# Attention, experts and a gated layer in one kernel: earlier weight loads, routing products in the score banks, one more copy on VectorE, and rows that hold columns and logits together

## The chip, the cores and the metric

The kernel runs on one core of a Trainium2 chip. The metric is device time in microseconds (us) of one execution. Five queues of instructions run side by side and each keeps its own order: TensorE (PE), VectorE (DVE), ScalarE (ACT), GpSimd (POOL) and SyncE (SP, which here only issues transfers). Instructions wait for each other through semaphores, so a late instruction holds everything behind it on its own queue.

## The reference

Three layers in a row, all in fp32:

```python
def _attn_ref(q, k, v, s):                      # B, H, S, D = 4, 8, 576, 64
    scores = scale * np.matmul(q, k.transpose(0, 1, 3, 2))
    cum = np.cumsum(np.maximum(s, 0.0), axis=-1)
    bias = -(cum[:, :, :, None] - cum[:, :, None, :])
    scores = np.where(causal, -1e9, scores + np.minimum(bias, 0.0))
    attn = np.exp(scores - scores.max(-1)); attn /= attn.sum(-1) + 1e-09
    return np.matmul(attn, v)
def _moe_ref(x, w_gate, w1, w2):                # 2304 tokens, 512 wide, 8 experts of 1024
    logits = x @ w_gate; expert_idx = np.argmax(logits, axis=1)
    ...                                         # gate_w: softmax of the chosen expert
    out[mask] = gate_w * (np.maximum(xe @ w1[e], 0.0) @ w2[e])
def _moe2_ref(x, w1, w2, w3, w_out):            # 768 wide
    return np.maximum(np.maximum(x @ w1, x @ w2), x @ w3) @ w_out
```

## The kernel before

The program has three stages. **Attention** goes over 16 pairs of heads (4 batches, 4 pairs each). Each pair has 576 query rows: four blocks of 128 for each of the two heads, and the last 64 rows of both heads together in one block of 128 partitions (the tiles `nst`, `Pt`, `tsum`). **The experts** follow: tokens are grouped by expert, gathered from the DRAM tensor `xd` and multiplied by weights that arrive in pieces of 128 x 1024 fp32; a piece is loaded (`wr`), rounded to its high half by ACT (L185) and the rest is taken by DVE (L681). **The second layer** comes last.

The order of the attention stage is written out as numbers. Every step is put into a heap at a slot by `at(slot, fn)`, and popping the heap writes the instructions; a slot is no time, only a place in the order. One pair has IT = 25 slots, and `SEQ` gives the place of each of its steps: `A0 B0 A1 B1 C2 C3 TT` are transposes of the exponentials into a PSUM bank "b" (L368) and their copies into `ptT` (L408 on DVE, L410 on ACT), `s0` to `s9` are scores into banks "a" (L302; L322 for the last rows), `v0 v1` are the products with the values into banks "c" (L420), `x0 x1` are the products with `rh` (L455), which give 128 columns of the output and 16 partial logits for each of five row tiles. There are 4 banks "a", 2 "b" and 2 "c", and each kind is used in turn, so a new product waits until the instruction that reads the bank's last product is done.

In a period PE works on three pairs: it transposes the exponentials of pair p-1 and multiplies them with the values, makes the scores of pair p, and makes the rows of pair p-2. DVE adds the bias and takes the minimum of each row (L308, L329), ACT takes the exponentials (L315, L337) out of three `ns` buffers. The bias of a pair, `bl` (two buffers), is loaded by SP from `cumd`, and POOL cuts the causal mask into it (L262, L267, L273).

After the last pair of each batch a list of some 33 small steps, `route`, follows at a spacing of RS slots. It sums the partial logits (L493), finds the expert, counts ranks by products with triangular and all-ones matrices (`r1`, L508 to L512, read by L516) and places token numbers by another product (`r3`, L539, read by L543). Both products of the first three batches use a bank "c".

Three weight pieces are placed inside the attention stage: `hi = WE1 + WES * n`, so at slots 80, 126 and 172, with the load WE0 slots from it and the rest (L681) WEL slots behind it.

Of the kernel before, what the change touches and what calls it, by code (L numbers as in the profile page):

```python
# [9 lines left out]
F32 = mybir.dt.float32  # L10
# [13 lines left out]
P = 128  # L24
WN = 128
# [32 lines left out]
BCE = "VAVAA"  # L58
LR, LE, LH, LL, LV, LK, LX = 2.5, 5.5, 1.5, 4.0, 1.0, 1.5, 1.5
NSB, PPB = 3, 4  # L60
# [14 lines left out]
WLO = "V"  # L75
WE0, WE1, WES, WEL, WEH = -15, 80, 46, 15, "A"
WHE, WLE = "A", "V"
# [13 lines left out]
       "v1": 9.1}  # L91
TDVE = ("A1", "B1")


def emit(nc, tc, qt, kt, v, s, wg, w1, w2, m64, out, dbg=None):
# [12 lines left out]
    cumd = dp.tile([B * H, BW], F32, name="cumd")  # L108
    xd = dp.tile([NT, DM], F32, name="xd")
    w32 = dp.tile([9, P, 1024], F32, name="w32")  # L110
# [12 lines left out]
    V.tensor_tensor_scan(cum, sn, sn, 0.0, ALU.add, ALU.max)  # L123
    cs = ab.tile([B * H, CW], F32, tag="hlv", name="cs", bufs=2)
# [4 lines left out]
    chl = ab.tile([B * H, 2, S], F32R, tag="hlv", name="chl", bufs=2)  # L129
    V.tensor_scalar(chl[:, 0], cum, 1.0, 1.0, ALU.mult, ALU.mult)  # L130
# [150 lines left out]
    xr = {}  # L281
    lp = {}

    def scores(p, slots):
# [76 lines left out]
        at(t + LE, tex)  # L361
        at(t + LE + 1, tnorm)

# [74 lines left out]
    def xrow(p, slots):  # L438
        d = st[p]
        b, h = divmod(2 * p, H)  # L440

        def begin():
            if h == 0:
                xr[b] = ab.tile([P, 5, DM], F32, tag="xr", name="xr", bufs=2)
                lp[b] = ab.tile([P, 5, H, NE], F32, tag="lp", name="lp", bufs=1)
                V.memset(lp[b][64:128, 4], 0.0)
            rc = d["rc"] = ab.tile([P, 5, 2], F32, tag="rc", name="rc", bufs=2)
            V.tensor_scalar(rc, ssum[b][:, :, h:h + 2], 1e-9, None, ALU.add)
            V.reciprocal(rc, rc)

        def mm(t0, t1):
            px = d["px", t0] = bank("c")
            for t in range(t0, t1):
                c = 144 * (t - t0)
                T.matmul(px[:, c:c + 144], d["oT"][:, 128 * t:128 * t + 128], rh[:, h // 2, :], start=True, stop=True)  # L455

        def ev(t0, t1):
            nt = t1 - t0
            pv = d["px", t0][:, :nt * 144].rearrange("p (t w) -> p t w", t=nt)
            for sl, ta, tb in (((slice(0, P)), t0, min(t1, 4)), ((slice(0, 64)), 4, t1)):  # L460
                if tb <= ta:
                    continue
                n = sl.stop
                pw = pv[sl, ta - t0:tb - t0]
                rr = d["rc"][sl, ta:tb, :].rearrange("p t (g o) -> p t g o", o=1)
# [12 lines left out]
    def route(b, t0):  # L478
# [25 lines left out]
        def r1():  # L504
            ohb = z["ohb"]
            z["pr"] = bank("b" if b == B - 1 else "c")
            prv = z["pr"][:, :5 * NG]
            T.matmul(prv, tri, ohb.rearrange("p t e -> p (t e)"), start=True, stop=False)  # L508
            for t in range(4):
                n = 4 - t  # L510
                T.matmul(prv[:, NG * (t + 1):], one, bc(ohb[:, t:t + 1, :], (P, n, NG)), start=False, stop=False)
            T.matmul(prv, one, bc(ocb.rearrange("p (o e) -> p o e", o=1), (P, 5, NG)), start=False, stop=True)  # L512

        op(r1)
        op(lambda: A.activation(sm([P, 5, NE], "ex"), z["ls"], AF.Exp))
        op(lambda: V.tensor_tensor(sm([P, 5, NG], "rv"), z["pr"][:, :5 * NG].rearrange("p (t e) -> p t e", t=5), oh,  # L516
# [39 lines left out]
    def constants():  # L556
        for g in range(2):
            V.tensor_copy(rh[64 * g:64 * g + 64, :, 64 * g:64 * g + 64],
                          bc(idf[64 * g:64 * g + 64, 64 * g:64 * g + 64].rearrange("p (o d) -> p o d", o=1), (64, H // 2, 64)))
        for tf, ti in late:  # L560
            V.tensor_copy(tf, ti)
# [17 lines left out]
    for g in range(2):  # L579
        at(6, lambda g=g: A.dma_start(rh[64 * g:64 * g + 64, :, 128 + 8 * g:136 + 8 * g],  # L580
                                        wg.rearrange("(h g d) e -> g d h e", g=2, d=64)[g]))
# [269 lines left out]
    def overflow():  # L851
        why = "bounded by the counts of the tokens"
        op = tc.alloc_tile_pool(name="op", bufs=1, side="right", reuse_waits="tile")
        with tc.If(nwin["n"] > 0):
            with tc.For_i(0, nwin["n"], 1) as i:
# [5 lines left out]
                SP.dma_start(ix, idd[ds(st_, WN)])  # L861
                x = op.tile([WN, DM], F32, name="x")
# [368 lines left out]
```

## Time and profile before

| | |
|---|---|
| median of 3 runs (lowest to highest) | 832.94 us (829.03 to 835.2) |
| the profiled execution | 829.74 us, of it a span of 827.9 us |
| PE busy | 765.1 us, 92% of the span |
| DVE, ACT, POOL busy | 431.1, 346.5, 110.9 us |
| PE busy from 0 to 240 us (attention and the change to the experts) | 200.0 of 240.0 us |
| PE busy from 240 us to the end | 565.1 of 587.9 us |

The attention stage ends at about 222 us. Up to there PE has holes; behind it PE is busy almost all the time. The profile names for each hole which engine's instruction ended it, and that is what has to be read.

### The profile page before, as it was taken

What the parts mean: (1) busy time and instruction counts of PE and PEld (TensorE: products, weight loads), DVE (VectorE), ACT (ScalarE), POOL (GpSimd) and SP (SyncE); (2) the same over time, 40 slices, a digit from 0 to 9 for tenths busy, and PEclk for the clock granted to TensorE, in tenths of its full rate; (3) what the DMA queues carried; (4) which work ended last, traced back from release to release, by engine and by line L of the source; (5) the groups of instructions that cost most, each with busy time, mean ns of one, the idle gap of its engine ahead of it and who ended that gap; (6) DMA issues with size and microseconds to landing.
All of it is one profiled execution on the core that took longest, in us unless ns stands there. A gap on an engine that the chain in (4) does not pass through costs nothing. (4 is left out here: it accounts for less than half of the span.)

```text
span 827.9 us, 13233 instructions
## 1 busy us (share of the span) xinstructions
PE 765.1 (92%) x4910; PEld 687.8 (83%) x4910; DVE 431.1 (52%) x1185; ACT 346.5 (42%) x804; POOL 110.9 (13%) x230
## 2 busy tenths in 40 slices
PE   7887778888889898898999999999999999999996
PEld 4565556556689898898899999998999999899995
DVE  5556465748567776777889944542222312223120
ACT  4766466567646444334554544522121211212111
POOL 3332132323412100200110000001000010100001
PEclk9999999999999999899999999999999999999998
DMA  6775856758258687867867742501000010100001
GB/s 177 204 187 144 238 126 177 193 162 238 78 185 290 229 282 257 283 228 255 295 232 240 228 152 81 178 2 38 1 26 13 1 39 1 38 1 9 30 1 39
DMA packets 36047, 115.47 MB, mean 139 GB/s; under 512 B 4921, under 2 KB 5003, under 8 KB 34059
## 3 DMA queue, kind: packets, MB, share of 16 engines
q1 hardware_dynamic: 25259, 85.27, 34.4%
q10 hardware_dynamic: 7456, 18.89, 6.5%
q0 software_dynamic: 3264, 10.42, 3.6%
q8 instruction: 40, 0.66, 0.3%
q14 instruction: 28, 0.23, 0.1%
HBM read 98.56 MB, written 16.01 MB: 138 GB/s over the span
## 5 line engine op out<-in xcount | busy, mean ns | idle before, releaser
L1127 DVE TENSOR_TENSOR mA<-ps_a,mA 128x384 f32<-128x384 f32 x72 | 40.2, 558 | 175.8 <-PE ps_a L935 175.8
L935 PE MATMUL ps_a<-yc,wq 128*128 128x384 f32 x720 | 126.9, 334 | 0.0
L935 PEld LDWEIGHTS ps_a<-yc,wq 128*128 128x128 f32 x720 | 125.2, 188 | 0.4
L935 PE MATMUL ps_c<-h,wq 128*128 128x336 f32 (+1 forms) x672 | 103.3, 310 | 9.5 <-ACT yT L981 5.5
L935 PEld LDWEIGHTS ps_c<-h,wq 128*128 128x128 f32 x672 | 97.9, 188 | 11.2 <-ACT yT L981 6.1
L935 PE MATMUL ps_a<-yc,wm 128*128 128x384 f32 x576 | 101.8, 334 | 0.0
L935 PE MATMUL ps_a<-xT,wq 128*128 128x336 f32 (+1 forms) x648 | 100.3, 314 | 0.1
L935 PEld LDWEIGHTS ps_a<-yc,wm 128*128 128x128 f32 x576 | 100.0, 188 | 0.0
L935 PEld LDWEIGHTS ps_a<-xT,wq 128*128 128x128 f32 x648 | 96.5, 193 | 0.4 <-DVE h L960 0.3
L315 ACT ACTIVATE P<-ns,mn 128x512 f32<-128x512 f32 (+3 forms) x128 | 70.6, 557 | 12.1 <-DVE mn L308 12.0
L935 PE MATMUL ps_c<-wm,g 128*128 128x512 f32 x324 | 74.7, 390 | 0.0
L1131 ACT ACTIVATE g<-mA 128x384 fp32r<-128x384 f32 x36 | 19.0, 527 | 132.9 <-DVE mA L1127 132.9
L935 PEld LDWEIGHTS ps_c<-wm,g 128*128 128x128 f32 x324 | 60.7, 188 | 12.4
L420 PE MATMUL ps_c<-ptT,nv 128*64 128x320 f32 (+4 forms) x448 | 50.8, 364 | 20.5 <-ACT ptT L410 19.2
L420 PEld LDWEIGHTS ps_c<-ptT,nv 128*64 128x64 f32 x448 | 29.6, 136 | 46.2 <-ACT ptT L410 27.0
L308 DVE CUSTOM_DVE_ANT_0 ns<-ps_a,bl 128x512 f32<-128x512 f32 (+3 forms) x128 | 57.4, 487 | 19.6 <-ACT P L315 9.3
L1150 POOL DMA_INDIRECT out<-o,midi x18 | 17.6, 976 | 373.3 <-ACT o L1146 366.3
L681 DVE TENSOR_TENSOR wq<-wr,wq 128x1024 fp32r<-128x1024 f32 x46 | 56.1, 1220 | 18.9 <-ACT wq L185 17.6
L185 ACT ACTIVATE wq<-wr 128x1024 fp32r<-128x1024 f32 x46 | 48.5, 1057 | 38.3 <-DMA wr<-in_w 33.9
L368 PE MATMUL ps_b<-idf,P 128*128 128x128 f32 x320 | 47.3, 288 | 8.0 <-ACT ptT L410 6.9
L410 ACT ACTIVATE ptT<-ps_b 128x512 f32<-128x512 f32 (+1 forms) x96 | 43.4, 505 | 19.3 <-PE ps_b L368 19.3
L302 PE MATMUL ps_a<-nk,nq 64*128 64x512 f32 (+3 forms) x256 | 48.1, 479 | 1.7 <-DVE mn L308 1.7
(222 smaller groups left out, 980.3 us busy)
## 6 DMA issues: line engine op xcount, KB each, us to landing
wr<-in_w SPq DMA_DIRECT2D x62, 512.0 KB, 4.6
bl<-cumd SPq DMA_DIRECT2D x30, 528.0 KB, 8.4
dr<-in_m ACTq DMA_DIRECT2D x24, 512.0 KB, 4.2
xr<-in_w SPq DMA_DIRECT2D x18, 512.0 KB, 3.9
nq<-in_qt SPq DMA_DIRECT2D x16, 352.0 KB, 3.4
nv<-in_v SPq DMA_DIRECT2D x16, 320.0 KB, 9.2
nk<-in_kt SPq DMA_DIRECT2D x16, 288.0 KB
w<-dc ACTq DMA_DIRECT2D x18, 256.0 KB, 4.7
```

The lines of the kernel that those rows point to most:

```text
L185: A.activation(o, x, AF.Copy)
L302: T.matmul(d["sp", i, g][:, :w], d["q"][r, 128 * i:128 * i + 128], d["k"][r, :w], start=True, stop=True)
L308: V.tensor_tensor_reduce(out=ns[:, :w], in0=d.pop(("sp", i, g))[:, :w], in1=d["bl"][:, 1024 * g + BOFF[i]:1024 * g + BOFF[i] + w], scale=- ...
L315: A.activation(pp, d.pop(("ns", i, g))[:, :w], AF.Exp, bias=d["mn"][:, c:c + 1], scale=-1.0, accum_out=ssum[b][:, i, h + g:h + g + 1])
L368: T.transpose(pt[:, c:c + 128], (d["P", "t"] if g == "t" else d["P", g, i])[:, k0:k0 + 128], idf)
L410: A.activation(f(d["pt"]), src, AF.Copy)
L420: T.matmul(po[64 * g:64 * g + 64, qa - c0:c1 - c0], d["v"][:, g, j], d["pt"][:, g, POFF[j] + qa - 128 * j:POFF[j] + c1 - 128 * j], start=( ...
L681: (V if eng == "V" else G).tensor_tensor(t[:, 1], raws.pop(key), t[:, 0].bitcast(F32), ALU.subtract)
L935: T.matmul(ps_, w_(zw), x_(zx), start=(first and n == 0), stop=(last and n == 2))
L1127: V.tensor_tensor(m, pm[:, :CH], m, ALU.max)
L1131: A.activation(t[:, 0], h2[c, f, "m"], AF.Copy)
L1150: G.indirect_dma_start(out, bass.IndirectOffsetOnAxis(ap=midi[:, n:n + 1].bitcast(U32), axis=0), h2.pop((c, x, "s")), None)
```

## The change

Four edits. The early weight pieces are loaded 62 slots ahead of their split in place of 15, and their rest is taken 3 slots behind it in place of 15. The routing products `r1` and `r3` of the first three batches go to a bank "a". The copy of `TT` (the last rows' transposes) is made by DVE in place of ACT. The row tile `xr` is 576 wide: for each pair of heads 8 logits, 128 columns, 8 logits; so one multiplication per bank takes columns and logits together, `lp` is gone, and the rows in `xd` and the gathered rows are 576 wide. The step that normalises the last rows stands 3.5 slots behind their exponential in place of 1. Three small tiles change the buffers that they share (`cs`, `chl`, `xw`).

```diff
+HW = 72
+XW = 8 * HW
-WE0, WE1, WES, WEL, WEH = -15, 80, 46, 15, "A"
+WE0, WE1, WES, WEL, WEH = -62, 80, 46, 3, "A"
-TDVE = ("A1", "B1")
+TDVE = ("A1", "B1", "TT")
-    xd = dp.tile([NT, DM], F32, name="xd")
+    xd = dp.tile([NT, XW], F32, name="xd")
...
-        at(t + LE + 1, tnorm)
+        at(t + LE + LN, tnorm)
...
-            pv = d["px", t0][:, :nt * 144].rearrange("p (t w) -> p t w", t=nt)
-            for sl, ta, tb in (((slice(0, P)), t0, min(t1, 4)), ((slice(0, 64)), 4, t1)):
...
-                V.tensor_tensor(xr[b][sl, ta:tb, 64 * h:64 * h + 128].rearrange("p t (g d) -> p t g d", g=2),
-                                pw[:, :, 0:128].rearrange("p t (g d) -> p t g d", g=2), bc(rr, (n, tb - ta, 2, 64)), ALU.mult)
-                V.tensor_tensor(lp[b][sl, ta:tb, h:h + 2, :], pw[:, :, 128:144].rearrange("p t (g e) -> p t g e", g=2), bc(rr, (n, tb - ta, 2, NE)),
-                                ALU.mult)
+            rr = d["rc"][:, t0:t1, :].rearrange("p t (g o) -> p t g o", o=1)
+            V.tensor_tensor(xr[b][:, t0:t1, HW * h:HW * h + 144].rearrange("p t (g w) -> p t g w", g=2),
+                            d["px", t0][:, :nt * 144].rearrange("p (t g w) -> p t g w", t=nt, g=2),
+                            bc(rr, (P, nt, 2, HW)), ALU.mult)
...
-        op(lambda: V.tensor_reduce(sm([P, 5, NE], "L"), lp[b].rearrange("p t h e -> p t e h"), AX.X, ALU.add))
+        for g, nm in enumerate(("L", "L1")):
+            o = g * (HW + D)
+            op(lambda o=o, nm=nm: V.tensor_reduce(
+                sm([P, 5, NE], nm), xr[b].rearrange("p t (m w) -> p t w m", w=2 * HW)[:, :, o:o + NE], AX.X, ALU.add))
+        op(lambda: V.tensor_tensor(z["L"], z["L"], z["L1"], ALU.add))
...
-            z["pr"] = bank("b" if b == B - 1 else "c")
+            z["pr"] = bank("b" if b == B - 1 else "a")
...
-            pg = z["pg"] = bank("b" if b == B - 1 else "c")
+            pg = z["pg"] = bank("b" if b == B - 1 else "a")
...
-                    T.transpose(pt[:, 0:WN], x[:, P * kk:P * kk + P], idf[0:WN, 0:WN])
+                    T.transpose(pt[:, 0:WN], heads(x, kk), idf[0:WN, 0:WN])
...
+    def heads(x, kk):
+
+        return x[:, 2 * HW * kk + NE:2 * HW * kk + NE + P]
```

How the order moves, at three places. **DVE, in the period in which the first batch's routing begins** (`ISA ns` is L308's minimum of a block, `ISA nst` that of the last rows, `mn` its read-out, `r_L` the logits). Before:

```order
L308 ISA ns,mn<-ps_a,bl 128x128
L308 ISA mn 128x1
L681 TENSOR_TENSOR wq_997<-wr_902,wq_997 128x1024
L494 TENSOR_REDUCE r_mx<-r_L 128x5
L495 TENSOR_TENSOR r_ls<-r_L,r_mx 128x40
L496 TENSOR_SCALAR r_val<-r_ls 128x40
L329 ISA nst,mn<-ps_a,bl 128x256
```

Now:

```order
L489 TENSOR_REDUCE r_L<-xr 128x40
L311 ISA ns,mn<-ps_a,bl 128x128
L311 ISA mn 128x1
L311 ISA ns,mn<-ps_a,bl 128x128
L311 ISA mn 128x1
L489 TENSOR_REDUCE r_L_1095<-xr 128x40
L491 TENSOR_TENSOR r_L<-r_L,r_L_1095 128x40
L411 COPY ptT<-ps_b 128x2x4x64
L492 TENSOR_REDUCE r_mx<-r_L 128x5
L332 ISA nst,mn<-ps_a,bl 128x256
```

The copy of `TT` stands between the last blocks' minima and the last rows' minima, in every period; in a period with routing, sums of logits stand ahead of it. The rest of the weight piece has left this place: it now stands ahead of the first minimum of the same period.

**PE, at the rank product of the second period of routing** (`rh,oT` are the row products, `nk,nq` the scores). Before:

```order
L508 LDWEIGHTS tri
L508 MATMUL ps_c<-r_ohb,tri 128x50
...
L512 LDWEIGHTS one
L512 MATMUL ps_c<-ocb,one 128x50
...
L455 MATMUL ps_c<-rh,oT 128x144 x5
L302 MATMUL ps_a<-nk,nq 128x384 x2
```

Now:

```order
L456 MATMUL ps_c<-rh,oT 128x144 x3
L506 LDWEIGHTS tri
L506 MATMUL ps_a<-r_ohb,tri 128x50
...
L510 LDWEIGHTS one
L510 MATMUL ps_a<-ocb,one 128x50
L456 MATMUL ps_c<-rh,oT 128x144 x2
L305 MATMUL ps_a<-nk,nq 128x384 x2
L305 MATMUL ps_a<-nk,nq 128x128 x2
```

The rank product left the ring of two banks "c" and entered the ring of four banks "a", in which the fourth score product behind it gets the same bank.

**SP, the loads ahead of the first weight piece.** Before, the piece stood here:

```order
L206 DMA nk_504<-in_kt 128x576
L206 DMA nq_506<-in_qt 128x704
L673 DMA wr0_594<-in_w1 128x1024
L211 DMA bl_637<-cumd_63 64x2112 x2
```

Now it stands two pairs earlier, behind the loads of the third pair (numbered 2) and ahead of that pair's bias:

```order
L210 DMA nk_249<-in_kt 128x576
L210 DMA nq_251<-in_qt 128x704
L671 DMA wr0_307<-in_w1 128x1024
L215 DMA bl_322<-cumd_63 64x2112 x2
```

The second and third pieces move up by the same distance.

## Rows read from the trace of the kernel before

**Rows 1.** The page's first part: busy us of each engine, share, instructions.

```profile
PE 765.1 (92%) x4910; PEld 687.8 (83%) x4910; DVE 431.1 (52%) x1185; ACT 346.5 (42%) x804; POOL 110.9 (13%) x230
```

**Rows 2.** Exponentials of the last rows, one per pair: min/median/max ns, first and last start.

```profile
L337 ACT ACTIVATE Pt<-nst,mn x16: 760/766/775, 17.2 to 222.5; 128x576 f32<-128x576 f32 x16
```

**Rows 3.** Stretches: us, then busy us (instructions) of each engine, clock, DMA share, GB/s.

```profile
17.20:29.90 12.70, 11.27 (x75) 7.35 (x74) 6.61 (x30) 8.46 (x27) 4.85 (x12) 1.00 0.95 257
42.40:57.20 14.80, 11.71 (x85) 8.03 (x84) 8.20 (x33) 9.39 (x28) 3.79 (x8) 1.00 0.72 174
69.60:84.70 15.10, 11.37 (x85) 7.72 (x84) 9.77 (x40) 9.33 (x29) 3.79 (x8) 1.00 0.64 162
84.70:118.80 34.10, 25.25 (x179) 17.89 (x178) 18.29 (x84) 17.97 (x55) 7.38 (x16) 0.95 0.63 173
143.50:158.40 14.90, 11.52 (x91) 7.95 (x90) 9.71 (x44) 8.51 (x29) 3.74 (x8) 1.00 0.77 220
171.60:183.90 12.30, 11.15 (x85) 7.75 (x84) 7.13 (x33) 8.40 (x28) 3.74 (x8) 1.00 0.60 166
```

**Rows 4.** Timeline of an undisturbed period: start, us, what, [idle before <-releaser].

```profile
178.94 1.14 PE L322 MATMUL ps_a<-nk,nq 128*128 128x256 f32 x4
...
179.09 0.29 DVE L308 CUSTOM_DVE_ANT_0 ns<-ps_a,bl 128x128 f32<-128x128 f32 x1 [0.18 <-ACT P L315]
179.30 0.08 DVE L308 DVE_READ_ACCUMULATOR2_ANT mn<- 128x1 f32 x1
...
179.57 0.42 DVE L329 CUSTOM_DVE_ANT_0 nst<-ps_a,bl 128x256 f32<-128x256 f32 x1 [0.18 <-PE ps_a L322]
...
180.57 0.60 ACT L410 ACTIVATE ptT<-ps_b 128x512 f32<-128x512 f32 x1
...
181.22 2.27 PE L420 MATMUL ps_c<-ptT,nv 128*64 128x320 f32 x20 [1.15 <-ACT ptT L410]
```

**Rows 5.** Waits of PE and ACT up to 240 us: total us, times, longest.

```profile
PE ps_c L420 <- ACT ptT L410: 19.2, 16, 1.5
PE ps_b L368 <- ACT ptT L410: 6.9, 2, 4.3
...
PE ps_c L455 <- DVE r_rv L516: 4.5, 2, 2.2
...
ACT wq L185 <- DMA wr<-in_w: 9.6, 3, 4.9
```

**Rows 6.** DVE's groups up to 240 us by shape: busy us, mean ns.

```profile
L408 DVE COPY ptT<-ps_b 128x384 f32<-128x384 f32 x32 | 15.8, 526 | 0.0
...
L466 DVE TENSOR_TENSOR xr<-ps_c,rc 128x384 f32<-128x384 f32 x16 | 8.8, 549 | 3.8 <-PE ps_c L455 3.7
...
L681 DVE TENSOR_TENSOR wq<-wr,wq 128x1024 fp32r<-128x1024 f32 x5 | 6.0, 1214 | 0.0
...
L493 DVE TENSOR_REDUCE r_L<-lp 128x40 f32<-128x320 f32 x4 | 3.0, 748 | 0.0
```

**Rows 7.** Timeline of the bias: SP's load, POOL's mask, DVE's first use; then the third pair's.

```profile
168.70 1.09 SPq L211 DMA_DIRECT2D bl<-cumd  x2
...
179.92 0.64 POOL L262 TENSOR_SCALAR_AFFINE_SELECT bl<-bl 128x512 f32<-128x512 f32 x1 [3.94 <-DMA bl<-cumd]
...
185.71 0.69 DVE L308 CUSTOM_DVE_ANT_0 ns<-ps_a,bl 128x512 f32<-128x512 f32 x1 [0.59 <-PE ps_a L302]
...
27.09 0.64 POOL L262 TENSOR_SCALAR_AFFINE_SELECT bl<-bl 128x512 f32<-128x512 f32 x1 [3.72 <-DMA bl<-cumd]
...
31.69 0.69 DVE L308 CUSTOM_DVE_ANT_0 ns<-ps_a,bl 128x512 f32<-128x512 f32 x1 [0.59 <-PE ps_a L302]
```

**Rows 8.** The tile r_ca (min/median/max ns), and POOL's mask beside its longest.

```profile
L531 DVE TENSOR_TENSOR r_ca<-ohA,r_dio x3: 316/316/609, 97.4 to 206.0; 128x150 fp32r<-128x150 f32 x3
...
205.80 0.64 POOL L262 TENSOR_SCALAR_AFFINE_SELECT bl<-bl 128x512 f32<-128x512 f32 x1 [5.07 <-DMA bl<-cumd]
...
206.00 0.61 DVE L531 TENSOR_TENSOR r_ca<-ohA,r_dio 128x150 fp32r<-128x150 f32 x1
```

More of the change, by code (lines that the diff above doesn't have):

```diff
@@ L58 @@
 BCE = "VAVAA"
-LR, LE, LH, LL, LV, LK, LX = 2.5, 5.5, 1.5, 4.0, 1.0, 1.5, 1.5
+LR, LE, LH, LV, LX, LN = 2.5, 5.5, 1.5, 1.0, 1.5, 3.5
 NSB, PPB = 3, 4
@@ L123, in emit @@
     V.tensor_tensor_scan(cum, sn, sn, 0.0, ALU.add, ALU.max)
-    cs = ab.tile([B * H, CW], F32, tag="hlv", name="cs", bufs=2)
+    cs = ab.tile([B * H, CW], F32, tag="xr", name="cs", bufs=2)
     sel = ab.tile([B * H, 256], F32R, tag="ns", name="sel", bufs=NSB)
@@ L128, in emit @@
     G.affine_select(sel, selx, pattern=[[-1, 2], [0, 128]], compare_op=ALU.is_equal, fill=0.0, base=0, channel_multiplier=1)
-    chl = ab.tile([B * H, 2, S], F32R, tag="hlv", name="chl", bufs=2)
+    chl = ab.tile([B * H, 2, S], F32R, tag="ptT", name="chl", bufs=1)
     V.tensor_scalar(chl[:, 0], cum, 1.0, 1.0, ALU.mult, ALU.mult)
@@ L281, in emit @@
     xr = {}
-    lp = {}
     def scores(p, slots):
@@ L443, in begin @@
             if h == 0:
-                xr[b] = ab.tile([P, 5, DM], F32, tag="xr", name="xr", bufs=2)
-                lp[b] = ab.tile([P, 5, H, NE], F32, tag="lp", name="lp", bufs=1)
-                V.memset(lp[b][64:128, 4], 0.0)
+                xr[b] = ab.tile([P, 5, XW], F32, tag="xr", name="xr", bufs=2)
             rc = d["rc"] = ab.tile([P, 5, 2], F32, tag="rc", name="rc", bufs=2)
@@ L458, in ev @@
             nt = t1 - t0
-            pv = d["px", t0][:, :nt * 144].rearrange("p (t w) -> p t w", t=nt)
-            for sl, ta, tb in (((slice(0, P)), t0, min(t1, 4)), ((slice(0, 64)), 4, t1)):
[L461 to L465, printed above, removed]
-                V.tensor_tensor(xr[b][sl, ta:tb, 64 * h:64 * h + 128].rearrange("p t (g d) -> p t g d", g=2),
-                                pw[:, :, 0:128].rearrange("p t (g d) -> p t g d", g=2), bc(rr, (n, tb - ta, 2, 64)), ALU.mult)
-                V.tensor_tensor(lp[b][sl, ta:tb, h:h + 2, :], pw[:, :, 128:144].rearrange("p t (g e) -> p t g e", g=2), bc(rr, (n, tb - ta, 2, NE)),
-                                ALU.mult)
+            rr = d["rc"][:, t0:t1, :].rearrange("p t (g o) -> p t g o", o=1)
+            V.tensor_tensor(xr[b][:, t0:t1, HW * h:HW * h + 144].rearrange("p t (g w) -> p t g w", g=2),
+                            d["px", t0][:, :nt * 144].rearrange("p (t g w) -> p t g w", t=nt, g=2),
+                            bc(rr, (P, nt, 2, HW)), ALU.mult)
         at(slots[0] - 0.5, begin)
@@ L512, in r1 @@
             T.matmul(prv, one, bc(ocb.rearrange("p (o e) -> p o e", o=1), (P, 5, NG)), start=False, stop=True)
+        C[-1] = lambda: A.activation(sm([P, 5, NE], "ex"), z["ls"], AF.Exp)
         op(r1)
-        op(lambda: A.activation(sm([P, 5, NE], "ex"), z["ls"], AF.Exp))
         op(lambda: V.tensor_tensor(sm([P, 5, NG], "rv"), z["pr"][:, :5 * NG].rearrange("p (t e) -> p t e", t=5), oh,
@@ L557, in constants @@
         for g in range(2):
-            V.tensor_copy(rh[64 * g:64 * g + 64, :, 64 * g:64 * g + 64],
+            V.tensor_copy(rh[64 * g:64 * g + 64, :, NE + D * g:NE + D * g + D],
                           bc(idf[64 * g:64 * g + 64, 64 * g:64 * g + 64].rearrange("p (o d) -> p o d", o=1), (64, H // 2, 64)))
@@ L579, in emit @@
     for g in range(2):
-        at(6, lambda g=g: A.dma_start(rh[64 * g:64 * g + 64, :, 128 + 8 * g:136 + 8 * g],
+        at(6, lambda g=g: A.dma_start(rh[64 * g:64 * g + 64, :, (HW + D) * g:(HW + D) * g + NE],
                                         wg.rearrange("(h g d) e -> g d h e", g=2, d=64)[g]))
@@ L861, in overflow @@
                 SP.dma_start(ix, idd[ds(st_, WN)])
-                x = op.tile([WN, DM], F32, name="x")
+                x = op.tile([WN, XW], F32, name="x")
                 G.indirect_dma_start(x, None, xd, bass.IndirectOffsetOnAxis(ap=ix.bitcast(U32), axis=0))
@@ L898, in gather @@
         if n == 0:
-            xw[n] = [ab.tile([P, DM], F32, tag=tag, name="xw" + tag, bufs=k) for tag, k in (("hlv", 2), ("r_cbo", 1))]
+            xw[n] = [ab.tile([P, XW], F32, tag=tag, name="xw" + tag, bufs=k) for tag, k in (("hlv", 1), ("r_cbo", 1))]
         else:
-            t = pools["hp"].tile([P, NWIN, DM], F32, tag="xw", name="xw", bufs=2)
+            t = pools["hp"].tile([P, NWIN, XW], F32, tag="xw", name="xw", bufs=2)
             xw[n] = [t[:, x] for x in range(NWIN)]
@@ L913, in xtr @@
             k = min(WN, cap[n] - WN * x)
-            T.transpose(pt[:, WN * x:WN * x + k], xw[n][x][0:k, P * kk:P * kk + P], idf[0:k, 0:k])
+            T.transpose(pt[:, WN * x:WN * x + k], heads(xw[n][x][0:k], kk), idf[0:k, 0:k])
     def act_tile(n, nm, i):
```

## The prediction

> **What bounds the kernel now.** I read the shares first. PE is busy 92% of the span, DVE 52%, ACT 42% [rows 1], so a hole in PE is the thing to look for. Nearly all holes lie ahead of 240 us, in attention. There I cut the time at the exponentials of the last rows, one per pair: the first starts at 17.2, the last at 222.5 us [rows 2], so 15 periods take 205.3 us, 13.7 each. An undisturbed one takes 12.3 and has 11.15 us of PE work (the stretch from 171.60 us) [rows 3]; most of the others agree with it, and the rest are longer: 14.8, 15.1, 34.1 for two, 14.9 [rows 3]. Against fifteen times 12.3 the excess is 20.8 us. So there are two things to explain: 1.15 us missing in every period, and 20.8 us in a few.
>
> The timeline of the undisturbed period shows the first [rows 4]. PE ends the last rows' scores at 180.08 and then stands until 181.22, because the copy of `TT` starts on ACT only at 180.57, behind four exponentials and one copy. The wait list has it 16 times, 19.2 us in all [rows 5]. DVE at that time has ended the last block's minimum at 179.38 and works on the last rows at 179.57. The same list holds the rest [rows 5]: ACT waits three times, 9.6 us in all, for a weight piece, which stops PE's copies behind it (6.9 us in two waits), and PE waits twice 2.2 us at the row products for the bank that the rank product holds.
>
> **The change part by part.**
>
> *The copy of TT on DVE.* A 128x384 copy there takes 0.526 us [rows 6]; ACT's copy of 512 took 0.60 [rows 4]. For 512 columns DVE needs at least 0.53 and, in proportion to the columns, at most 0.70; I take 0.66, near the upper end, since the multiplication of the same 384 columns takes 0.549 [rows 6]. Placed behind the read-out at 179.38 it ends at 180.04, and PE, 0.05 us behind (as now: 181.17 to 181.22), starts at 180.1 where its own work ends at 180.08. The hole goes, and PE is next in line itself: 1.1 us a period, 15 times, **-16.5 us**. Bounds: nothing, if DVE is late; 19.2, the whole wait. What DVE does later by 0.6, the last rows' minima, is not needed before ACT's exponential 2 us later; it also frees the bias buffer later (third rival).
>
> *The weight pieces.* SP issues them two periods earlier, so the 9.6 us of waiting go. What stays are ACT's split and DVE's rest, 1.21 us each time [rows 6], at new places. First piece (stretch from 42.40, excess 2.5): the rest now stands between the two DVE copies for which PE's next transposes wait; I charge 0.9 of its 1.2, and 0.3 for the split ahead of the exponentials. 2.5 becomes 1.2: **-1.3**. Second (69.60, excess 2.8): the rest stands ahead of the first minimum and delays DVE up to the copy of TT by 1.3; in the same period the sums of logits (below) stand ahead of that copy, 1.0. 2.8 becomes 2.3: **-0.5**. Third, with the first batch's routing (84.70 to 118.80, excess 34.1 - 24.6 = 9.5): there remain the rank product, 0.5 of PE (14.9 - 12.3 - 2.2 is 0.4), its bank 0.9 (below), the placing product 0.7, and the piece 1.6, its split ahead of the exponential and its rest ahead of the placing product's input. 9.5 becomes 3.7: **-5.8**.
>
> *Routing in the score banks.* The row products no longer wait, but the fourth score product behind the rank product takes its bank, and the reader on DVE now stands behind both row multiplications. Bounds: 0, if the bank is read in time; 2.2, as now. PE now has two row products and three score products to do before it needs the bank, where it had none, so I take less than the middle: 0.9. In the second batch's period (143.50) 2.6 becomes 0.5 + 0.9: **-1.2**. The third batch's rank product stands elsewhere and waits now as little as before: 0.
>
> *Rows with columns and logits.* Per pair DVE makes two multiplications in place of six; none of the six is waited for closely, the saving is some 0.3 us and off the path: 0. The sum of logits is now two reductions of half the size and an addition, where one took 0.748 [rows 6]. They stand ahead of TT's copy, which no longer has 1.15 us of cover. I charge 1.0 (0.75 if only elements count, 1.5 if each costs as the one did), in the periods of the second and third batch, which were undisturbed so far: **+2.0**. Rows in DRAM are one eighth longer; the stores have a whole batch's time, and the gathers are issued while PE still has other work: 0.
>
> *The rest.* The first piece goes ahead of the third pair's bias while DMA is busy 0.95 of the time at 257 GB/s (the stretch from 17.20 us) [rows 3]: 0.5 MB there are 2 us. That bias's mask ends at 27.73 and is used at 31.69 [rows 7], 4.0 us of cover, less 1.1 for each period that got shorter and these 2 us. It just holds; I charge **+0.2**, with 0 and 2 as bounds. Behind the last pair the TT copy gains **-0.3**. Three tiles in other buffers and the later normalising of the last rows (its first user on PE is half a period away): 0. What follows attention keeps its order and moves as a whole.
>
> Sum: -16.5 - 1.3 - 0.5 - 5.8 - 1.2 + 2.0 + 0.2 - 0.3 = **-23.4 us**. From the profiled execution's 829.74 that is 806.3; it lies 3.2 below the median of the three runs, from which it would be 809.5. I forecast between the two: **808**.
>
> **Rivals.**
>
> *The gain of TT's copy is lost on DVE* (0.08). DVE's last block minimum already waited 0.18 us for ACT to free a buffer [rows 4], so DVE is not free to run ahead. If the copy ends 1.1 us later than I have it, PE stands as before and only the other terms are left: -6.9, **823**. Against it: DVE works 7.1 of 12.3 us.
>
> *The experts take part of it back* (0.10): PE then meets weight pieces or gathered rows that are not there. For: the DMA queues carry more in that stage. Against: their loads wait for buffers that PE itself frees, and so move with it. I price it at a third of the gain: **816**.
>
> *Slower: the bias comes too late* (0.03). It is issued at 168.70, when the last rows' minima of the pair two before free the buffer, and its mask starts at 179.92, ended by that DMA: 11.2 us. It is first used at 185.71, 5.15 us behind the mask's end [rows 7]. The change takes 1.1 from each of the two periods between and issues it 0.5 later: 2.5 left. A load of more than 13.7 us stalls DVE, half a microsecond per period for each further one; at 16.8 us the 23.4 are gone, and at 18.5 the kernel takes 806.3 + 15 x 2.4 = **842**. For: loads now share DMA with weights earlier, and the same bytes pass in less time. Against: at 0.95 DMA share the third pair's load still landed in time [rows 7].
>
> *DVE and POOL hold each other up* (0.14). One tile of DVE with both inputs in SBUF took 0.609 us in place of 0.316 while POOL cut a mask from 205.80 on [rows 8]. The second piece's rest has both inputs in SBUF and now begins 2.3 us into its period, beside POOL's normalising of the last rows. If it waits for that, I let DVE lose the rest's own 1.2 us once more: **809.2**, inside the range. The Trainium skill says this ("SBUF — State Buffer", section "SBUF: two separate sides"): a VectorE instruction with two SBUF inputs and a GpSimd instruction that reads SBUF exclude each other for a whole instruction, and the loser blocks. The row agrees in direction; it shows 0.29 us, less than the whole of POOL's 0.64.
>
> One more rule of the skill speaks against moving the copy: "VectorE: DVE Perf Modes", specifications, has ScalarE closer to PSUM and VectorE closer to SBUF. Its table of costs gives 120 cycles and one per column at 0.96 GHz for a VectorE copy out of PSUM, an estimate of 0.66 us, against ScalarE's row of 0.60; by either the copy ends where PE's own work does, and the sum stays.
>
> **How the numbers follow.** The forecast's own case has 0.62, and 0.03 is left for what I don't see. Its unknown costs (bank 0 to 2.2 twice, sums 0.75 to 1.5 three times, TT 0 to 19.2 around 16.5, the pieces) put it between 800 and 815. The range **800 to 820** takes in the second and fourth rival, some 0.82 in all. About 1% can be told from no change in this kernel, so faster means under 824.6: all cases but the third and a part of the first, **0.92**; within 1% **0.05**; slower **0.03**.
>
> **What would show it.** PE's wait for `ptT` from ACT falls from 19.2 to under 3 us and comes back only in the periods with routing or a weight piece, as a wait for DVE's copy. The undisturbed period is 11.2 to 11.3 us. ACT never waits for a weight piece. PE's wait for `r_rv` moves from the row products to the scores and is near 1 us, twice. The last pair's exponential starts at about 199 us in place of 222.5, and from there to the end the time is as before. I am wrong if the undisturbed period stays above 11.8, or if the stretch behind attention grows.

## The result and the profile after

Four runs of the changed kernel have a median of 806.08 us (803.23 to 806.8), the kernel before beside them 834.07 us: a ratio of 0.966, with a 95% interval from 0.959 to 0.972. Six later runs, timed beside others of the kernel before, gave 804.49 us, a ratio of 0.971 (0.967 to 0.975). The forecast was 808 us. The profiled execution took 806.8 us, its span 805.0; the times in this section are from it.

The page's first part, which answers to [rows 1], and the exponentials of the last rows, which answer to [rows 2]:

```profile
PE 764.0 (95%) x4910; PEld 687.8 (85%) x4910; DVE 437.5 (54%) x1141; ACT 338.3 (42%) x788; POOL 108.0 (13%) x230
```

```profile
L340 ACT ACTIVATE Pt<-nst,mn x16: 763/766/775, 16.4 to 197.4; 128x576 f32<-128x576 f32 x16
```

PE does the same work in a span that is 22.9 us shorter. The last exponential starts at 197.4 in place of 222.5 us, the first at 16.4 in place of 17.2, so the 15 periods of attention take 181.1 in place of 205.2 us. All of the gain is there: from the last exponential to the end it is 607.6 us, against 605.4 before.

Windows from exponential to exponential, with the columns of [rows 3]: the first period, the one with the first piece, with the second piece and the sums of logits, with the third piece and the first batch's routing (two periods), with the second batch's rank product, and an undisturbed one:

```profile
16.40:28.63 12.23, 10.83 (x77) 7.13 (x76) 7.03 (x30) 7.94 (x26) 3.70 (x8) 1.00 1.02 278
...
39.76:51.78 12.02, 11.41 (x86) 7.74 (x85) 8.60 (x31) 8.98 (x28) 3.77 (x8) 1.00 0.81 220
62.91:76.14 13.23, 11.58 (x86) 7.84 (x85) 10.62 (x38) 9.00 (x28) 3.73 (x8) 1.00 0.83 227
76.14:102.78 26.64, 23.67 (x180) 16.62 (x179) 19.12 (x79) 16.94 (x54) 7.41 (x16) 1.00 0.71 198
125.61:138.51 12.90, 11.86 (x92) 8.26 (x91) 9.88 (x41) 8.06 (x28) 3.93 (x7) 1.00 0.90 256
151.08:162.21 11.13, 11.13 (x86) 7.77 (x85) 7.34 (x29) 7.93 (x27) 3.73 (x8) 1.00 0.68 173
```

In the last row PE's busy time is the whole period: in an undisturbed period PE is now the bound itself. The two periods of the third piece show one thing more. PE's work there took 25.25 us before, at a mean granted clock of 0.95 [rows 3], and takes 23.67 us now, at 1.00. Before, PE waited 4.3 us on account of the late third piece, and just behind that wait, from 106.9 to 110.2 us, the granted clock was 0.50, the lower of TensorE's two levels (1.2 and 2.4 GHz). So 1.6 of the 7.5 us gained there is PE's own work at the full clock. The same 0.50 comes back in several runs below.

Period by period against the forecast (its price laid on 12.31 - 1.1 = 11.2 us for each period):

| us | before | forecast | after |
|---|---|---|---|
| undisturbed (4th, 12th), each | 12.31 | 11.2 | 11.13 |
| 3rd, first piece | 14.89 | 12.4 | 12.02 |
| 5th, second piece and sums | 15.13 | 13.5 | 13.23 |
| 6th and 7th, third piece and routing | 34.15 | 26.1 | 26.64 |
| 9th and 13th, sums of logits, each | 12.31 | 12.2 | 11.70 |
| 10th, second batch's rank product | 14.93 | 12.6 | 12.90 |
| all 15 | 205.2 | 182.2 | 181.1 |

The timeline of the undisturbed period, which answers to [rows 4]:

```profile
158.40 1.14 PE L325 MATMUL ps_a<-nk,nq 128*128 128x256 f32 x4
158.55 0.29 DVE L311 CUSTOM_DVE_ANT_0 ns<-ps_a,bl 128x128 f32<-128x128 f32 x1 [0.43 <-ACT P L318]
158.76 0.08 DVE L311 DVE_READ_ACCUMULATOR2_ANT mn<- 128x1 f32 x1
158.76 0.69 DVE L411 COPY ptT<-ps_b 128x512 f32<-128x512 f32 x1
...
159.37 0.41 DVE L332 CUSTOM_DVE_ANT_0 nst<-ps_a,bl 128x256 f32<-128x256 f32 x1
...
159.50 2.27 PE L423 MATMUL ps_c<-ptT,nv 128*64 128x320 f32 x20
```

PE's own work ends at 159.54, the copy at 159.45. The products with the values follow with no gap; before they stood 1.15 us. Note how close it is: the copy ends 0.05 us ahead of the products' start, so it has almost no slack.

The waits up to 240 us, which answer to [rows 5]:

```profile
PE ps_c L423 <- DVE ptT L411: 5.3, 10, 1.3
...
DVE wq L679 <- ACT wq L189: 4.4, 3, 2.2
...
PE ps_a L537 <- DVE mn L311: 2.1, 2, 1.7
ACT wq L189 <- DMA wr<-in_w: 2.0, 1, 2.0
...
PE ps_a L305 <- DVE r_rv L514: 1.6, 2, 0.8
```

The wait for ACT's copy of `TT` (19.2 us) has become ten short ones for DVE's. The one wait of ACT for a piece lies behind attention; the three early ones (9.6 us) are gone. Two rows are new: DVE waits for ACT's split (two of the three times in attention), since the rest now stands right behind it in the order, and PE waits at the placing product (L537) for a score bank.

DVE's groups up to 240 us by shape, which answer to [rows 6]:

```profile
L411 DVE COPY ptT<-ps_b 128x384 f32<-128x384 f32 x32 | 15.9, 527 | 0.0
L679 DVE TENSOR_TENSOR wq<-wr,wq 128x1024 fp32r<-128x1024 f32 x11 | 13.6, 1239 | 4.4 <-ACT wq L189 4.4
...
L411 DVE COPY ptT<-ps_b 128x512 f32<-128x512 f32 x16 | 10.9, 680 | 0.0
...
L461 DVE TENSOR_TENSOR xr<-ps_c,rc 128x432 f32<-128x432 f32 x16 | 9.6, 600 | 3.6 <-PE ps_c L456 3.6
...
L489 DVE TENSOR_REDUCE r_L<-xr 128x40 f32<-128x160 f32 x8 | 3.4, 425 | 0.0
```

And the third pair's bias, which answers to the end of [rows 7]: its mask, and its first use.

```profile
28.79 0.63 POOL L266 TENSOR_SCALAR_AFFINE_SELECT bl<-bl 128x512 f32<-128x512 f32 x1 [5.53 <-DMA bl<-cumd]
...
30.41 0.69 DVE L311 CUSTOM_DVE_ANT_0 ns<-ps_a,bl 128x512 f32<-128x512 f32 x1 [0.58 <-PE ps_a L305]
```

The mask ends at 29.42, 0.99 us ahead of its use: of 4.0 us of cover 1.0 is left. It "just holds", and DVE's idle time there is still ended by PE's scores.

### The profile page after: what moved, and what is told of

Same layout as the page of the kernel before. It is cut to its first block, busy times and chain, and to the rows that moved or that the text cites. A ratio compares the mean times of both kernels' runs of the same rounds, so it can differ in the third digit from the quotient of the medians.

```text
span 805.0 us, 13198 instructions
## 1 busy us (share of the span) xinstructions
PE 764.0 (95%) x4910; PEld 687.8 (85%) x4910; DVE 437.5 (54%) x1141; ACT 338.3 (42%) x788; POOL 108.0 (13%) x230
## 5 line engine op out<-in xcount | busy, mean ns | idle before, releaser
L937 PEld LDWEIGHTS ps_c<-wm,g 128*128 128x128 f32 x324 | 60.7, 188 | 12.4
L423 PEld LDWEIGHTS ps_c<-ptT,nv 128*64 128x64 f32 x448 | 29.5, 136 | 31.2 <-DVE ptT L411 13.5
L958 ACT ACTIVATE h<-ps_a 128x336 fp32r<-128x336 f32 (+1 forms) x64 | 27.6, 432 | 51.7 <-PE ps_a L937 51.3
```

Source lines behind the costliest of these rows:

```text
L423: T.matmul(po[64 * g:64 * g + 64, qa - c0:c1 - c0], d["v"][:, g, j], d["pt"][:, g, POFF[j] + qa - 128 * j:POFF[j] + c1 - 128 * j], start=( ...
L937: T.matmul(ps_, w_(zw), x_(zx), start=(first and n == 0), stop=(last and n == 2))
L958: A.activation(t[:, 0, :c], hT[n, f, "p"][:, :c], AF.Relu)
```

## The experiments

One table first, all from the profiles (one execution each), in us. The first period stands apart, since it ranged from 11.4 to 15.0 in kernels alike there: it depends on when attention starts (16.4 to 17.2 us) and when the second pair's bias lands, and in f3, f4, k1, k2 and k3 the granted clock fell to 0.50 in it, so that PE's work took 12.3 us in place of 10.8 to 11.2. The last column gives the ratio of times to the kernel before on the same chip.

| kernel | first period | other 14 | behind attention | ratio (95%) |
|---|---|---|---|---|
| before | 12.6 | 192.6 | 605.4 | |
| f1: TT alone | 11.4 | 185.5 | 606.8 | 0.990 (0.982 to 0.998) |
| f2: pieces alone | 12.5 | 184.9 | 604.2 | 0.992 (0.987 to 0.996) |
| f3: banks alone | 13.8 | 193.1 | 605.3 | 1.003 (0.999 to 1.008) |
| f4: rows alone | 15.0 | 194.1 | 605.8 | 0.999 (0.996 to 1.003) |
| k1: TT and pieces | 13.7 | 174.1 | 610.8 | 0.981 (0.972 to 0.990) |
| k2: k1 and banks | 13.6 | 170.2 | 603.5 | 0.973 (0.968 to 0.978) |
| changed | 12.2 | 168.8 | 607.6 | 0.966 (0.959 to 0.972) |
| changed, again (a0) | 12.1 | 170.1 | 602.5 | 0.971 (0.967 to 0.975) |
| k3: load ahead of the copy | 13.9 | 176.7 | 599.6 | 0.978 (0.967 to 0.990) |
| k4: load behind the minima | 11.6 | 168.6 | 601.7 | 0.972 (0.959 to 0.985) |
| b1: pieces moved | 12.3 | 165.8 | 605.2 | 0.965 (0.957 to 0.974) |
| b1, again | 12.2 | 165.3 | 604.2 | 0.964 (0.960 to 0.968) |
| b2: b1, sums moved | 11.4 | 162.6 | 601.9 | 0.963 (0.959 to 0.967) |

**Each part alone.** f1 is the kernel before with one name more:

```diff
-TDVE = ("A1", "B1")
+TDVE = ("A1", "B1", "TT")
```

> The kernel before with one edit: the copy of TT on DVE. Theory A (PE stood 1.15 us a period for ACT's copy and is next in line itself): the undisturbed period falls from 12.3 to 11.2 us, the time by 13 to 17 us, to about 815 in a run like the profiled one of before (829.7); the waits for weight pieces (ACT, 9 to 10 us) and for the rank product's bank (2.2 us, twice) stay. Rival (the copy only pays together with the shorter row multiplications on DVE): the period stays above 11.8 and the time falls by under 7 us. If the stretch behind the last pair's exponential (605.4 us before, 607.6 now) grows here by 2 us too, the loss there comes with an earlier end of attention; if it stays at 605, it comes from the order that the routing's extra step moves.

f1 took 823.46 us. The undisturbed period is 11.13 us, as in the changed kernel, but the gain is 7.1 us over the 14 periods and not 15. ACT's wait for the pieces in f1:

```profile
ACT wq L185 <- DMA wr<-in_w: 10.5, 3, 4.9
```

It was 9.6 us [rows 5]. A piece still is issued 15 slots ahead of its split and takes 5.4 to 7.9 us from issue to split in the two kernels, so shorter periods leave ACT no less to wait. The two periods of the first and second piece even grew, the 3rd from 14.9 to 15.3 us and the 5th from 15.1 to 17.6:

```profile
39.95:55.29 15.34, 13.32 (x85) 9.18 (x84) 8.89 (x34) 9.00 (x28) 3.77 (x8) 0.89 0.62 166
66.43:84.06 17.63, 13.03 (x85) 9.07 (x84) 10.54 (x41) 8.87 (x28) 3.77 (x8) 0.90 0.61 174
```

Before, the same 85 products took 11.7 and 11.4 us at a clock of 1.00 [rows 3]. In f1 the granted clock was 0.50 from 48.6 to 51.9 and from 72.5 to 75.9 us, soon behind waits of PE of 1.7 and 3.2 us. That makes about 3 of the 8 us that are missing, and no list of waits shows it. In the 9th, 10th and 13th period 0.7 us each is lost to steps of the routing that stand on DVE ahead of the copy.

f2 is the kernel before with the other line of numbers:

```diff
-WE0, WE1, WES, WEL, WEH = -15, 80, 46, 15, "A"
+WE0, WE1, WES, WEL, WEH = -62, 80, 46, 3, "A"
```

> The kernel before with one edit: the three early pieces loaded 62 slots ahead, their rest 3 slots behind the split. Theory A: ACT waits at most once and briefly for a piece, the three long periods shrink by 7 to 10 us in sum, 820 to 823. Rival (the rest's new place on DVE costs about what the wait did): 826 or more, with PE waiting for DVE's copies in the same periods.

f2 took 822.37 us. No wait of ACT for a piece is left in attention; the wait for the copy of `TT` is there as before (19.5 us, 16 times), and so are 4.5 us for `r_rv`. The gain is 7.7 us over the 14 periods.

f3 is the kernel before with the routing products in banks "a":

```diff
-            z["pr"] = bank("b" if b == B - 1 else "c")
+            z["pr"] = bank("b" if b == B - 1 else "a")
...
-            pg = z["pg"] = bank("b" if b == B - 1 else "c")
+            pg = z["pg"] = bank("b" if b == B - 1 else "a")
```

> The kernel before with one edit: rank and placing products of the first three batches in the score banks. Theory A (a wait of 2.2 us at the row products becomes one of about 0.9 at the scores, twice): 2 to 3 us less, 827. Rival (the wait only moves): within 1 us of before.

f3 took 833.32 us, no difference that can be told. The two waits of 2.2 us at the row products are gone and the second batch's period fell from 14.9 to 13.7 us. But PE's wait behind the late second piece grew from 2.6 to 3.5 us, and here the granted clock fell behind it, as it did not before: PE's work in the 5th period took 13.0 in place of 11.4 us. The wait behind the third piece stayed (4.3 us before, 4.5 here), again with a low clock behind it. So the traces have the late pieces take what the bank gave; how much of that comes back in every execution, one trace cannot tell.

f4 is the changed kernel with those three edits undone, so it keeps the wide rows, their multiplications and sums, the later normalising and the extra routing step. It also keeps a move that the list of edits leaves out: the exponential of the routing stands a step ahead of the rank product in place of behind it.

> The changed kernel with the other three edits taken back: rows that hold columns and logits, and the later normalising step. Theory A (DVE's saving is off the path, the split sums are covered by the 1.15 us that PE stands for TT): within 1.5 us of before. Rival (the six multiplications were felt, since banks come free earlier): 4 us less or better. If the stretch behind the last pair's exponential grows by 2 us here, the extra routing step and the longer rows are its cause.

f4 took 830.59 us, no difference that can be told.

**Two and three parts together.** k1 is f1 and f2 in one, k2 adds f3.

> The kernel before with the copy of TT on DVE and the early weight pieces at their new places, and with nothing else of the change (bank choice, rows and routing are those of before). Alone the two took 8.3 and 7.8 us off attention (from the first to the last pair's exponential), 16.1 together, and the whole change took 24.1. Theory (they need each other: a weight piece landed at a fixed time of DMA, so shorter periods only made ACT wait longer for it, and with the pieces early the whole 1.15 us of each period comes through): attention 181 to 185 us, the excess of the two long periods that f1 had (17.6 and 20.0) gone, time 807 to 811. Rival (the sum of the two singles, and the rest of the gain needs the banks or the rows): attention near 189 us, time about 815.

k1 took 813.9 us, and 187.8 us of attention: between the two theories, nearer the rival. Over the 14 periods the gain is 18.5 us, where the singles give 14.8. Of the difference, 4.1 us stand in the 3rd and 5th period, where f1 had the late pieces and the low clock; the 10th takes 1.1 us back, since the clock fell there in k1. The whole times do not show this surplus: 0.990 times 0.992 is 0.982, and k1 has 0.981. The first period was 1.1 us longer than before, and so was PE's work in it (12.3 in place of 11.2 us, at a clock of 0.88). What the theory left out is in the list of waits of k1: the two for `r_rv` stand there as before.

```profile
PE ps_c L455 <- DVE r_rv L516: 4.5, 2, 2.2
```

> The kernel before with the copy of TT on DVE, the early weight pieces and the routing products in the score banks, so all of the change but the rows that hold columns and logits. Without the banks attention took 187.8 us, with all of the change 181.1. Theory (banks are worth 1.4 us of bank wait in each of two batches once the other holes are gone, and free the row products of the rest): attention 183 to 185.5; the rest, about 2 to 4 us, is the rows'. Rival (the rows matter little, as the change of them alone did not shorten the time): attention about 181 to 182.

k2 took 806.87 us, attention 183.8. The banks, worth nothing alone, give 3.9 us over the 14 periods once the pieces are early, and the same row of waits is gone. Of this, 2.8 us stand in the 10th period: 1.3 of them are PE's work, which had the low clock behind the wait for `r_rv` in k1 (13.1 us) and has the full one here (11.8). The rows then give 1.4 us (against a0, which has a low clock in its 7th period, under 0.2), nearly all of it in one period, the 14th. k2's timeline of DVE in the third batch shows a part of it:

```profile
183.99 0.17 DVE L525 TENSOR_TENSOR r_dio<-io,r_dd 128x15 f32<-128x15 f32 x1
184.07 0.82 DVE L528 TENSOR_TENSOR r_cbo<-io,r_bb 128x640 fp32r<-128x640 f32 x1
184.81 0.68 DVE L408 COPY ptT<-ps_b 128x512 f32<-128x512 f32 x1
```

`r_cbo` stands ahead of the copy of `TT`, and PE waits 0.79 us. In the changed kernel the routing has one step more, and the same instruction has slid behind the copy:

```profile
182.09 0.68 DVE L411 COPY ptT<-ps_b 128x512 f32<-128x512 f32 x1
182.69 0.81 DVE L526 TENSOR_TENSOR r_cbo<-io,r_bb 128x640 fp32r<-128x640 f32 x1
```

PE waits 0.13 us there, and the period is 11.61 in place of 13.10 us. The other half of the gain is the rank product. In k2 it takes a bank "a" and stands ahead of four score products, which take twice as long as in k1, where it takes a bank "c" (first line k2, second k1):

```profile
176.99 1.39 PE L302 MATMUL ps_a<-nk,nq 64*128 64x256 f32 x4
```

```profile
181.28 0.70 PE L302 MATMUL ps_a<-nk,nq 64*128 64x256 f32 x4
```

In the changed kernel the rank product stands behind those score products. So the gain in that period goes with places in the order, not with the wider rows' cheaper multiplications.

**Place or load on DVE.** k3 and k4 add one DVE reduction per period over 512 columns of `rh`, whose result is not used. k3 has it ahead of the copy of `TT`:

```diff
+            if u == "TT" and p < NP - 1:
+                V.tensor_reduce(ab.tile([P, 1], F32, tag="dum", name="dum", bufs=2), rh.rearrange("p m w -> p (m w)")[:, 0:512], AX.X, ALU.add)
```

k4 has the same line behind the minima of the last rows:

```diff
+            if x == 1 and p > 0:
+                V.tensor_reduce(ab.tile([P, 1], F32, tag="dum", name="dum", bufs=2), rh.rearrange("p m w -> p (m w)")[:, 0:512], AX.X, ALU.add)
```

> The changed kernel with one more DVE reduction over 512 columns of an SBUF tile (its result is not used) right ahead of DVE's copy of TT, for all pairs but the last. Reductions of 160 and 320 elements took 0.425 and 0.748 us, so it takes at least 0.55 and at most 1.15 us. Theory (the copy stands on PE's path with no cover left: it ends about 0.06 us ahead of PE's need): each of 15 periods grows by the reduction's own time less at most 0.1, an undisturbed one from 11.13 to 11.6 to 12.2; time 7 to 16 us more. Rival (DVE has room there because it idles 0.43 us just ahead of the last block's minimum, and 0.18 behind the copy): the growth is under 0.3 us a period, under 5 us in all.

k3 took 809.87 us (two runs). The reduction took 0.675 us, and the undisturbed period is 11.73: 0.60 us more, the whole of it less 0.08. The timeline of such a period:

```profile
165.94 0.68 DVE L410 TENSOR_REDUCE dum<-rh 128x1 f32<-128x512 f32 x1
166.53 0.68 DVE L413 COPY ptT<-ps_b 128x512 f32<-128x512 f32 x1
...
167.27 1.03 PE L425 MATMUL ps_c<-ptT,nv 128*64 128x320 f32 x6 [0.57 <-DVE ptT L413]
```

> The changed kernel with the same DVE reduction, now right behind the minima of the last rows, where DVE waits for about 2.5 us in an undisturbed period. Theory (not DVE's load but its place counts): undisturbed period stays at 11.13 to 11.2, time 0 to 2 us more, the costs falling in the periods with a weight piece or routing. Rival (DVE is the next bound as a whole, at 7.1 us and more of 11.1 busy): every period grows by 0.3 us or more, time 5 us and more longer.

k4 took 804.8 us (two runs), attention 180.2. The same instruction took 0.681 us and the undisturbed period is 11.13 us; in no other period does it cost more than 0.13 us against the first trace of the changed kernel. With two runs each the ratios of k3 and k4 overlap, so it is the periods of the traces that tell them apart, and these leave no room for the rival: here DVE's load does not bind, its place does.

**Moving what is left.** b1 changes the same line of numbers:

```diff
-WE0, WE1, WES, WEL, WEH = -62, 80, 46, 3, "A"
+WE0, WE1, WES, WEL, WEH = -44, 68.5, 25, 3.5, "A"
```

> The changed kernel with the three early weight pieces at other places: split by ACT at slots 68.5, 93.5 and 118.5 in place of 80, 126 and 172 (where ACT waits for PE ahead of its copy of oT), the rest 3.5 slots behind, where DVE waits behind the last rows' minima, loaded 44 slots ahead in place of 62, all three ahead of the first batch's routing. Theory (a split of 1.1 us and a rest of 1.2 us cost only where they stand ahead of PE's next copies or scores): the periods with pieces, now 12.0, 13.2 and 13.9 us (the last with routing), fall to 11.1 to 11.5 and the routing ones to 12.5 to 13, attention 4 us shorter at about 177, time about 802 to 803. Rival (ACT and DVE have no such room, or the pieces come later than their splits): the costs of about 1 us a piece move to other periods and the time stays within 1 us of the changed kernel.

b1 took 800.4 us. The 3rd period is 11.13, the 5th 11.75, the 6th 12.90 us (12.02, 13.23 and 13.85 in the changed kernel), attention 178.1. The bet was 4 us in attention; it is 3.

> The kernel with the pieces at slots 68.5, 93.5 and 118.5 once more, beside the changed kernel on the same chip. If its trace is right (178.1 us of attention in place of 181.1), it is 3 us faster than the changed kernel, and the piece periods are 11.1 to 11.8. If the earlier time (800.4) was the chip's, the two are within 1 us.

> The changed kernel itself once more, as the base for the two others timed beside it. Every theory: attention 180 to 182 us, ratio to the kernel before 0.96 to 0.975. What it tells apart: behind attention the changed kernel's trace took 2.2 us more than that of before. If the experts' stage gives back a part of the gain, this repeat again has 607 us or more there; if that was scatter of that stage (in the other runs it took 600 to 611 us), it lies anywhere between.

On one chip b1 took 800.1 us (796.34 to 801.62), the changed kernel 804.49 (801.58 to 808.87). Attention took 177.5 against 182.2 us, of which 1.6 us is the 7th period of the repeat (14.41 us, 12.79 in the first trace). Both traces of the changed kernel have PE wait 1.68 us at the placing product there; in the repeat the granted clock was 0.50 from 93.4 to 96.8 us behind it, and the same 84 products took 12.49 in place of 10.87 us. In b1 that wait is 0.45 us, and no period of attention has a low clock. Behind attention the repeat took 602.5 us. With k3 and k4 the same order there took 607.6, 602.5, 599.6 and 601.7 us (mean granted clock of the whole execution 0.990, 0.995, 0.996 and 0.996), on both sides of the 605.4 of before (0.991): the 2.2 us more of the first trace were scatter, not a part of the gain given back.

b2 moves the sums and the rank product's reader in `route`:

```diff
-            at(t0 + (RS, RS, RS2, RSL)[b] * i, f)
+            o = (RS, RS, RS2, RSL)[b] * i
+            if b < B - 1 and 2 <= i <= 6:
+                o = 10.7 + 0.02 * (i - 2)
+            if b < 2 and i == 14:
+                o = 24.6
+            at(t0 + o, f)
```

> As b1, and for the first three batches the sums of logits stand on DVE behind the last rows' minima in place of ahead of the copy of TT, and for the first two the reader of the rank product stands between the two row multiplications in place of behind both. Theory (place counts, since DVE idles about 2.5 us behind the last rows' minima): PE's waits for the copy of TT there (0.6, 0.9 and 0.5 us) go, and the two waits of 0.80 us for the bank become about 0.4; attention 2.0 to 3.0 us shorter than b1's, about 175.5, time about 798. Rival (the chain of the routing is late then: the rank product waits for the experts chosen, or the placing product's input comes later): the waits appear at r_ohb or r_ca, and the time is that of b1.

b2 took 797.13 us (794.77 to 801.48), attention 174.0; without the first period it is 2.7 to 3.2 us less than b1. PE's waits up to 240 us:

```profile
PE ps_c L423 <- DVE ptT L411: 3.0, 7, 1.3
PE ps_a L537 <- DVE mn L311: 0.9, 2, 0.5
PE ps_a L305 <- DVE r_rv L514: 0.7, 2, 0.3
```

The three waits at the sums are gone and the periods there are 11.13 us; the bank's wait fell from 0.80 to 0.35 us, twice. No new wait at `r_ca` came; the one at `r_ohb`, 0.5 us in the last batch, b1 has too. b2 is the fastest version by the medians, 7.4 us below the changed kernel on the same chip, and its slowest run lies just under the fastest of the changed kernel.

## Why the prediction was right, point by point

*The copy of TT.* Priced at 0.66 us, it took 0.680. The undisturbed period was given as 11.2 to 11.3 and is 11.13. f1 shows it for the copy alone, k3 that the copy has 0.08 us of slack, as the argument that it ends where PE's own work ends had it. The Trainium skill's table of costs ("VectorE: DVE Perf Modes", section "The TRN2 errata — SBUF-src ops pay a fixed extra latency per instruction") led to an estimate of 0.66 us for this copy; the measured 0.680 is 3% above.

*The pieces.* The waits of ACT went, and what was left stands where the text put it: 0.9 of the 1.2 us given for the first piece, 2.1 of 2.3 for the second (the sums in it), 4.4 of 3.7 for the third with the routing. The last is the largest miss of a single term. The text did not see that 1.6 us of what the third piece cost before was PE's work at the low clock; that went together with the wait. The text named the rest as standing ahead of the placing product's input; it did not see that DVE would stand idle for ACT's split first, nor that the placing product, now in the ring "a", needs a bank that the minimum behind that rest frees:

```profile
90.07 1.23 DVE L679 TENSOR_TENSOR wq<-wr,wq 128x1024 fp32r<-128x1024 f32 x1 [1.66 <-ACT wq L189]
...
92.05 0.69 DVE L311 CUSTOM_DVE_ANT_0 ns<-ps_a,bl 128x512 f32<-128x512 f32 x1
```

```profile
92.80 0.73 PE L537 MATMUL ps_a<-r_ca,r_cbo 128*128 128x30 f32 x5 [1.68 <-DVE mn L311]
```

In b1, without a rest there, the same wait is 0.45 us.

*The banks.* Forecast 0.9 us of wait, twice; measured 0.81 and 0.80.

*The sums of logits.* Forecast +1.0 us in each of two periods, measured 0.57. The work itself is as priced (two reductions of 0.425 us and an addition of 0.20), but the first reduction fell into the 0.43 us that DVE otherwise idles ahead of the last block's minimum, which the price left out.

*What was left out, and what was luck.* The third batch's 14th period gained 1.5 and not 1.1 us, since `r_cbo` and the rank product got other places. The terms hold only with the other edits made, and so they were priced; as what each edit does by itself they do not hold. Alone, TT gives 7.1 us over 14 periods and not 15, and the banks and the rows nothing; only the pieces, with 7.7 us, come near their price (7.6). That the sum, 806.3 us, meets the profiled execution's 806.8 to half a microsecond is in part luck: the prices of single periods are off by up to half a microsecond both ways, and while attention began 0.8 us earlier and was 1.1 us shorter than forecast, the stretch behind it was 2.2 us longer than before.

*The rivals.* TT's gain was not lost on DVE, nor was the bias too late (0.99 us were left). The stretch behind attention grew by 2.2 us in the first trace, which the text named as a sign of being wrong; the repeat, k3 and k4 have less there than before, so a part of the gain given back by the experts is not shown. DVE and POOL holding each other up did occur, and twice. The second piece's rest took 0.2 us longer:

```profile
64.70 1.42 DVE L679 TENSOR_TENSOR wq<-wr,wq 128x1024 fp32r<-128x1024 f32 x1 [0.59 <-ACT wq L189]
```

The other two rests took 1.22 and 1.23 us; POOL was normalising the last rows from 64.31 on, for 1.73 us. Later in the same period the addition of the sums, also with both inputs in SBUF, met POOL's mask, right ahead of the copy of `TT`:

```profile
72.10 0.63 POOL L266 TENSOR_SCALAR_AFFINE_SELECT bl<-bl 128x512 f32<-128x512 f32 x1 [3.48 <-DMA bl<-cumd]
...
72.20 0.58 DVE L491 TENSOR_TENSOR r_L<-r_L,r_L 128x40 f32<-128x40 f32 x1
```

It took 0.58 in place of 0.20 us, and PE waited 1.19 us for the copy. In the repeat the mask came at 72.92, behind the addition; PE waited 0.81 us, and the period was 12.85 in place of 13.23 us. So this rival, in the first trace, cost PE 0.38 us at a place that the text had not named.

The difference of 2 to 3.5 us between the forecast of 808 and the medians (806.1, then 804.5) is within the scatter of the runs.

## What to carry to other kernels

Price the parts of a change in the state in which the others are made, and do not expect the parts alone to add up: in the traces a late transfer took back a part of what a copy or a bank gave, and two edits that measured nothing alone were worth 4 to 5 us on top of the others. Look at the granted clock of each period before you put a difference down to an order: PE's work behind a wait took 1.3 to 1.6 us more in some executions and not in others, one and the same kernel included. On an engine that is two thirds busy, look at each instruction ahead of the one that the bounding engine waits for: 0.68 us there cost about 0.6 in nearly every period, the same instruction where the engine idles cost next to nothing. Once the main hole is closed, list what else stands ahead of that instruction and move it into the idle stretch; that gave 7 us more here, with three edits to slots.

## What the runs showed of the hardware

A DVE instruction with both inputs in SBUF and POOL's work slow each other by amounts that vary with how they meet. In b1 the first rest met POOL's masks:

```profile
38.98 1.71 DVE L679 TENSOR_TENSOR wq<-wr,wq 128x1024 fp32r<-128x1024 f32 x1 [0.63 <-ACT wq L189]
...
39.65 1.44 POOL L277 TENSOR_SCALAR_AFFINE_SELECT bl<-bl 64x64 f32<-64x64 f32 x2
```

Alone they take 1.22 and 0.54 us, so DVE lost 0.49 and POOL 0.90. In b2, with the same places, no rest took more than 1.28 us, but POOL lost more:

```profile
38.70 1.23 DVE L684 TENSOR_TENSOR wq<-wr,wq 128x1024 fp32r<-128x1024 f32 x1 [0.62 <-ACT wq L189]
...
38.75 1.67 POOL L266 TENSOR_SCALAR_AFFINE_SELECT bl<-bl 128x512 f32<-128x512 f32 x1 [5.72 <-DMA bl<-cumd]
```

That mask alone takes 0.64 us. The Trainium skill ("SBUF — State Buffer", section "SBUF: two separate sides") has a VectorE instruction with two SBUF inputs and a GpSimd instruction that reads SBUF exclude each other for a whole instruction, the one that starts first going ahead. These masks agree: each ended 0.4 to 0.5 us behind the rest that it met. The normalising does not: it began 0.39 us ahead of the second rest and runs for 1.73 us, and the rest lost 0.2 us.

Behind some waits of PE the granted clock fell from 1.00 to 0.50, the lower of its two levels, for a while: in the kernel before behind a wait of 4.3 us, in f1 behind 1.7 and 3.2 (among others), in k1 behind 1.4 and 2.2, in the repeat of the changed kernel behind 1.7. PE's work in such a period took 1.3 to 1.6 us longer. The first trace of the changed kernel has the same waits of 1.4 and 1.7 us and no fall, and before, one of 2.6 us had none; the traces do not show what decides it.
